# FFN and score products issued as 32-column array tiles, squares on ScalarE, and gains as rows, in a fused attention and FFN kernel

## The chip, the cores and the metric

The kernel runs on one core of one Trainium2 chip. The metric is the device time of one execution in microseconds (us), and lower is better. The kernel before takes 411.36 us, the median of 11 runs that lie between 408.41 and 414.82. A core has TensorE (matrix products; PE in the profile, with its weight loads as PEld), VectorE (DVE), ScalarE (ACT), GpSimd (POOL) and SyncE (SP, which here only starts transfers). DMA queues move data between the chip's memory and the core's buffer, SBUF. Products land in PSUM banks, from which VectorE or ScalarE take them.

## The reference, cut to what matters

```python
# q, k, v: (8, 12, 448, 64); g_q, g_k: (64,)
q_n, k_n = rmsnorm(q, g_q), rmsnorm(k, g_k)      # x / sqrt(mean(x*x) + 1e-6) * g
attn = softmax(q_n @ k_n.T / 8)                  # per batch and head
x = (attn @ v).transpose(0, 2, 1, 3).reshape(3584, 768)
a, b = x @ w1, x @ w2                            # (768, 1024) each
out = (a * b @ w3) @ w_out                       # (1024, 1024), (1024, 768)
```

All inputs and the output are 32-bit floats. Sums of squares, scales and the score exponentials are needed for every one of 96 heads; the FFN runs over 3,584 tokens.

## The kernel before, in words

**Work units.** The kernel takes four heads at a time, a *quad*: 8 batches of 3 quads, 24 quads in all. A quad takes four steps (the code's slots, `sl` 0 to 3), numbered t = 4 * quad + sl. The 448 tokens of a head stand as 112 partitions x 4. w3 and w_out are first multiplied into one matrix, w34, so that the FFN is (a * b) @ w34.

**Preparing a quad** happens up to twelve steps ahead. `load_qk` loads q and k on SP's queue (quad 0's k on ScalarE's). `prep_sq` squares q and k, in two halves of two heads: on ScalarE for quads 0 to 4 (`N_SQ_ACT = 5`), on GpSimd (L159) for the 19 others. `prep_red` sums the squares on VectorE (L166), `prep_alpha` makes exp(-0.5 ln(.)) of the sums on ScalarE (L176, L177), and `prep_scale` multiplies on VectorE: q by alpha (qtmp, L188), that by the product of the gains (L195), k by alpha (L201). The scaled halves are transposed into qkT, by TensorE for quads 0 to 4 (`N_PE_T = 5`), by a DMA transpose on SP's queue for the rest.

**A step** then does three things on TensorE. `qk_exp` makes two score tiles (sc, L235), each of two heads, as two matmuls of 64 rows by 112 columns, one in the upper and one in the lower half of the array; ScalarE makes the exponential P of each score tile (L244). sc has two PSUM buffers, so the scores of a step wait for the exponentials of the step before. `pv_set` (L259), in steps 0 to 2 of the quad that follows, makes the row sums (kind 0) or half of the value product, as four 32-column array tiles side by side, one per head, in four rounds of 448 columns. From kind 0 ScalarE makes the reciprocal r (L269, L271); VectorE multiplies kinds 1 and 2 by r into xT (L275). Last come up to two *fillers*: in steps 1 to 13 transposes of w3 (L293) and pieces of w34 (wps, L301), later units of the FFN. `ffn1_a` (pa, L315) is six matmuls of 128 x 128 against 448 columns, taken out by ScalarE as a_sb (L323); `ffn1_b` (pb, L332) is six more, multiplied with a_sb by VectorE into abT (L339). `ffn2` (po, L354) is eight matmuls against 384 columns, copied by VectorE to o_sb (L361) and stored by SP. All of these but sc share four PSUM buffers (`mm_psum`). What is left of the FFN after the last quad runs by itself at the end.

**Order.** Nothing is scheduled by a program: the order in which the code issues instructions is the order on each engine. The table `PREP` with `SHIFT` says at which step each part of a quad's preparation is issued; from quad 7 on, the squares of quad n are issued at steps 4n - 9 and 4n - 8, behind that step's exponentials, r and a_sb, the alphas one step later. `W34_SLOTS` says how many pieces of w34 stand in a step, and `LAG` how far the second half of w34's columns is behind the first.

**The start.** Sixteen matmuls on zeros warm TensorE (L393). ScalarE's queue loads quad 0's k in two halves, and then g_q and g_k, each spread to 112 partitions (L403, L404); VectorE multiplies them and by 8 into g_b (L417, L418) ahead of its first reduction. GpSimd waits in a copy (`gate`, L408) for the last half of k and then issues the weights' loads on its own, software queue: both halves of w_outs' first columns, four parts of w3s, v of quad 0, the rest of w_outs. Further loads (`wq`) follow, four issued per step.

## Time and profile before

| | |
|---|---|
| median of 11 runs | 411.36 us (408.41 to 414.82) |
| the profiled execution's own time | 410.86 us |
| its span, from the first to the last instruction | 408.7 us |
| TensorE, VectorE, ScalarE, GpSimd busy | 382.4, 288.0, 249.9, 117.4 us |
| PE instructions (matmuls and weight loads) | 6,080 |
| pa, pb, po, sc, pv matmuls | 384, 384, 448, 384, 1,152 |
| squares on ScalarE, on GpSimd | 20, 76 |
| granted TensorE clock, mean | 0.978 |
| first score exponential starts | 18.25 us |
| first FFN matmul starts | 70.9 us |

An engine's busy time is the union of its instructions' times. A weight load and a matmul are two instructions; matmuls overlap in the array, so the mean time of one (355 ns for 448 columns) is longer than the distance from one start to the next. "The chain that ended last" is followed back from the last instruction, at each point to what released it. Rows name the kernel's line, the engine, and what is written from what is read.

### The profile page before, as it was taken

Reading aid. Unit: us, or ns where it says so; the run is one execution under the profiler, and the core shown is the slowest. Engines: PE = TensorE matmul, PEld = TensorE weight load, DVE = VectorE, ACT = ScalarE, POOL = GpSimd, SP = SyncE. Lnnn points to the kernel's source line nnn. Section 1 sums busy time; section 2 is a strip of 40 time slices with the busy share of each in tenths; the row PEclk is TensorE's granted clock in tenths of the full one; section 3 lists DMA queues with packets and bytes.
Section 4 is the critical chain, followed back from the end, with each engine's and each line's share of the span. In section 5 each row is a group of like instructions: output and inputs, shape, how many; then the busy total and the mean of one; then the engine's idle time right before and its main releaser. Section 6 shows DMA issues by size and latency. Waiting matters only on the chain.

```text
span 408.7 us, 7530 instructions
## 1 busy us (share of the span) xinstructions
PE 382.4 (94%) x3040; PEld 177.3 (43%) x3040; DVE 288.0 (70%) x383; ACT 249.9 (61%) x391; POOL 117.4 (29%) x135
## 2 busy tenths in 40 slices
PE   5299999999999899998999899899999999999995
PEld 1155554444444344434444343344444444445552
DVE  0676767988978878779888878878978973234232
ACT  2479888776677646665677565674767657751210
POOL 4233434444055405504323422422532500000000
PEclk9559999999999999999999999999999999999999
DMA  6999998367795568564886487556767652003004
GB/s 198 219 233 234 197 211 153 78 103 149 189 197 79 114 149 206 112 142 67 196 170 124 80 218 120 110 136 98 191 146 155 94 143 58 0 2 115 2 19 137
DMA packets 78530, 54.61 MB, mean 134 GB/s; under 512 B 38048, under 2 KB 72352, under 8 KB 78496
## 3 DMA queue, kind: packets, MB, share of 16 engines
q1 hardware_dynamic: 61568, 41.30, 43.1%
q0 software_dynamic: 16192, 12.32, 21.2%
q10 hardware_dynamic: 736, 0.52, 0.4%
q8 instruction: 24, 0.39, 0.4%
q14 instruction: 10, 0.08, 0.1%
HBM read 46.72 MB, written 11.01 MB: 141 GB/s over the span
## 4 chain that ended last, share of the span: by engine, by line
PE 76%; DVE 10%; ACT 5%; issue 5%; DMA 3%; ACTq 0%; DVEq 0%
PE pa L315 17%; PE pb L332 16%; PE po L354 16%; PE pv L259 13%; PE sc L235 9%; PE wps L301 4%; DVE qtmp L188 2%; DMA gk_b<-in_g_k_dram 2%; DVE qks L195 2%; DVE qks L201 2%; ACT P L244 2%; ACT sq L157 1%; DVE xT L275 1%; DMA out_dram<-o_sb 1%; PE w3T_ps L293 1%
## 5 line engine op out<-in xcount | busy, mean ns | idle before, releaser
L244 ACT ACTIVATE P<-sc 112x896 bf16<-112x896 f32 x192 | 165.5, 914 | 83.6 <-PE sc L235 83.6
L159 POOL TENSOR_TENSOR sq<-q_sb 112x512 f32<-112x512 f32 x38 | 41.9, 1104 | 166.5 <-DMA q_sb<-in_q_dram 122.2
L332 PE MATMUL pb<-xT,w2s 128*128 128x448 bf16 x384 | 83.1, 352 | 2.4 <-DVE xT L275 2.4
L315 PE MATMUL pa<-xT,w1s 128*128 128x448 bf16 x384 | 84.0, 354 | 1.0 <-DVE xT L275 1.0
L354 PE MATMUL po<-w34s,abT 128*128 128x384 bf16 x448 | 78.5, 327 | 4.8 <-DVE abT L339 4.8
L339 DVE TENSOR_TENSOR abT<-pb,a_sb 128x448 bf16<-128x448 f32 x64 | 39.7, 620 | 58.5 <-PE pb L332 58.2
L166 DVE TENSOR_REDUCE ssq<-sq 112x16 f32<-112x1024 f32 x48 | 58.0, 1209 | 5.0 <-ACT sq L157 5.0
L235 PE MATMUL sc<-qkT 64*112 64x448 bf16 x384 | 58.3, 380 | 1.3 <-DVE qkT L223 0.7
L354 PEld LDWEIGHTS <-abT 128*128 128x128 bf16 x448 | 41.2, 98 | 41.4 <-issue 10.2
L323 ACT CAST a_sb<-pa 128x448 bf16<-128x448 f32 x64 | 33.9, 529 | 36.2 <-PE pa L315 36.2
L332 PEld LDWEIGHTS <-w2s 128*128 128x128 bf16 x384 | 37.6, 98 | 39.2 <-issue 4.5
L315 PEld LDWEIGHTS <-w1s 128*128 128x128 bf16 x384 | 33.0, 98 | 45.1 <-issue 20.3
L201 DVE TENSOR_TENSOR qks<-k_sb,alpha 112x512 bf16<-112x512 f32 x48 | 52.3, 1090 | 0.0
L188 DVE TENSOR_TENSOR qtmp<-q_sb,alpha 112x512 bf16<-112x512 f32 x48 | 45.9, 957 | 6.1 <-ACT alpha L177 6.0
L361 DVE COPY o_sb<-po 128x384 f32<-128x384 f32 x56 | 30.4, 553 | 25.2 <-PE po L354 25.1
L259 PE MATMUL pv<-P,v_sb 112*32 112x448 bf16 x768 | 45.1, 355 | 0.0
L159 POOL TENSOR_TENSOR sq<-k_sb 112x512 f32<-112x512 f32 x38 | 42.8, 1126 | 3.5 <-DMA k_sb<-in_k_dram 3.5
L195 DVE TENSOR_TENSOR qks<-qtmp,g_b 112x512 bf16<-112x512 bf16 x48 | 37.2, 774 | 1.7
L235 PEld LDWEIGHTS <-qkT 64*112 64x112 bf16 x384 | 17.7, 127 | 33.0 <-issue 31.1
L275 DVE TENSOR_TENSOR xT<-pv,r 128x448 bf16<-128x448 f32 x48 | 29.5, 614 | 3.6 <-PE pv L259 3.6
L259 PEld LDWEIGHTS <-v_sb 112*32 112x32 bf16 x768 | 16.1, 96 | 24.0 <-issue 15.7
L301 PE MATMUL wps<-w_outs,w3T 128*128 128x384 bf16 x128 | 24.1, 339 | 0.0
(36 smaller groups left out, 183.5 us busy)
## 6 DMA issues: line engine op xcount, KB each, us to landing
q_sb<-in_q_dram SPq DMA_DIRECT2D x23, 448.0 KB, 5.4
k_sb<-in_k_dram SPq DMA_DIRECT2D x23, 448.0 KB, 6.2
v_sb<-in_v_dram POOLq DMA_DIRECT2D x24, 224.0 KB, 4.1
out_dram<-o_sb SPq DMA_DIRECT2D x8, 336.0 KB, 3.3
out_dram<-o_sb SPq DMA_DIRECT2D x8, 288.0 KB, 2.9
w3s<-in_moe_w_dram POOLq DMA_DIRECT2D x8, 256.0 KB, 14.2
out_dram<-o_sb SPq DMA_DIRECT2D x8, 240.0 KB, 3.9
w_outs<-in_moe_w_out_dram POOLq DMA_DIRECT2D x4, 384.0 KB, 13.1
```

What stands on the lines that cost most here:

```text
L159: nc.gpsimd.tensor_tensor(out=sq[:, t], in0=src[:, hs], in1=src[:, hs], op=MULT)
L166: nc.vector.tensor_reduce(out=s["ssq"][:, :, hs, :], in_=s.pop(("sq", pr)), axis=AX, op=ADD)
L188: nc.vector.tensor_tensor(out=qtmp.transpose([0, 2, 1, 3]), in0=s["q"][:, hs], in1=alpha[:, 0, hs].unsqueeze(3).broadcast_to([NP, 2, J, D] ...
L195: nc.vector.tensor_tensor(out=qks[:, 0], in0=qtmp, in1=g_b.unsqueeze(1).unsqueeze(1).broadcast_to([NP, J, 2, D]), op=MULT,)
L201: nc.vector.tensor_tensor(out=qks[:, 1].transpose([0, 2, 1, 3]), in0=s["k"][:, hs], in1=alpha[:, 1, hs].unsqueeze(3).broadcast_to([NP, 2, ...
L235: nc.tensor.matmul(out=sc[:, u, 0:S], lhsT=qkT[u * D : (u + 1) * D, pr, J + jk, :], rhs=qkT[u * D : (u + 1) * D, pr, 0:J, :].rearrange("d ...
L244: nc.scalar.activation(out=P[:, 2 * pr : 2 * pr + 2, jk, :], in_=sc[:, :, 0:S], func=AF.Exp)
L259: nc.tensor.matmul(out=ps[h * HALF : (h + 1) * HALF, :], lhsT=w, rhs=P[:, h, jk, :], start=(jk == 0), stop=(jk == J - 1), tile_position=(0 ...
L301: nc.tensor.matmul(out=ps[:, 0:NH], lhsT=w3T[:, gc, fc * 128 : (fc + 1) * 128], rhs=w_outs[:, gc, nh * NH : (nh + 1) * NH], start=(gc == 0 ...
L315: nc.tensor.matmul(out=ps[:, 0:S], lhsT=w1s[:, c, fi * 128 : (fi + 1) * 128], rhs=xT[b][:, c, :], start=(c == 0), stop=(c == CM - 1),)
L332: nc.tensor.matmul(out=ps[:, 0:S], lhsT=w2s[:, c, fi * 128 : (fi + 1) * 128], rhs=xT[b][:, c, :], start=(c == 0), stop=(c == CM - 1),)
L354: nc.tensor.matmul(out=ps[:, 0:NH], lhsT=abT[bp][:, fi, t * 128 : (t + 1) * 128], rhs=w34s[:, fi, nh * NH : (nh + 1) * NH], start=(fi == 0 ...
```

## The change

The FFN's matmuls (pa, pb, po) are issued as four matmuls each, on the four 32-column tiles of the array, with the same moving operand; each has its own weight load. The scores are issued likewise, as tiles of 64 rows by 32 columns (the last 16 wide): a pair of heads takes eight matmuls and not two. The products that make w34, and the transposes on TensorE, stay whole. All squares go to ScalarE (`N_SQ_ACT = 24`), so that GpSimd is left with loads. The gains are loaded as one row each; VectorE multiplies them after its first reduction, a matmul with a column of ones spreads the row to 112 partitions, and VectorE copies it to g_b. GpSimd's gate waits for the first half of q. The loads on its queue come in another order (`LOADS_0`, `LOADS_1`: o is a half of w_outs' columns, in two loads, w a part of w3s, v a quad's v), and `LAG` goes from 4 to 8, so that all first halves of w34 are made ahead of the second ones. Five quads go through TensorE's transposes, as before; loads of q and k on SP keep their places.

```diff
-    N_SQ_ACT = 5
+    N_SQ_ACT = 24
-    LAG = 4
+    LAG = 8
+    LOADS_0 = ["o0", "w0", "w1", "w2", "v0", "w3", "w4"]
+    LOADS_1 = ["w5", "v1", "w6", "w7", "o1", "v2"]
+    GATE = ("q", 0)
+    QK1_AT = -1
...
-    gq_b = const.tile([NP, D], FP, name="gq_b")
-    gk_b = const.tile([NP, D], FP, name="gk_b")
+    g_row = const.tile([1, 2, D], FP, name="g_row")
+    gp_row = const.tile([1, D], BF, name="gp_row")
+    ones_row = const.tile([1, NP], BF, name="ones_row")
...
             for u in range(2):
-                nc.tensor.matmul(
-                    out=sc[:, u, 0:S],
-                    lhsT=qkT[u * D : (u + 1) * D, pr, J + jk, :],
...
+                for c0 in range(0, NP, 32):
+                    c1 = min(c0 + 32, NP)
+                    nc.tensor.matmul(
+                        out=sc[c0:c1, u, 0:S],
+                        lhsT=qkT[u * D : (u + 1) * D, pr, J + jk, c0:c1],
...
+                        tile_position=(u * D, c0),
+                    )
...
+    def narrow(ps, n, lhsT, rhs, start, stop):
+        for h in range(4):
+            nc.tensor.matmul(
+                out=ps[32 * h : 32 * h + 32, 0:n],
+                lhsT=lhsT[:, 32 * h : 32 * h + 32],
+                rhs=rhs,
+                start=start,
+                stop=stop,
+                tile_position=(0, 32 * h),
+            )
+
     def ffn1_a(b, fi):
         ps = mm_psum.tile([128, 512], FP, tag="mm", name="pa")
         for c in range(CM):
-            nc.tensor.matmul(
-                out=ps[:, 0:S],
-                lhsT=w1s[:, c, fi * 128 : (fi + 1) * 128],
-                rhs=xT[b][:, c, :],
-                start=(c == 0),
-                stop=(c == CM - 1),
+            narrow(
+                ps, S, w1s[:, c, fi * 128 : (fi + 1) * 128], xT[b][:, c, :],
+                c == 0, c == CM - 1,
             )
...
-        nc.scalar.dma_start(out=gq_b, in_=g_q.unsqueeze(0).broadcast_to([NP, D]))
-        nc.scalar.dma_start(out=gk_b, in_=g_k.unsqueeze(0).broadcast_to([NP, D]))
+        nc.scalar.dma_start(out=g_row[:, 0], in_=g_q.unsqueeze(0))
+        nc.scalar.dma_start(out=g_row[:, 1], in_=g_k.unsqueeze(0))
...
-        nc.gpsimd.tensor_copy(out=gate, in_=st[0]["k"][:, HQ - 1, 0, 0:1])
-        load_wout(0, 0)
-        load_wout(0, 1)
-        for c in range(4):
-            load_w3(c)
-        load_v(0)
-        load_wout(1, 0)
-        load_wout(1, 1)
+        if GATE is not None:
+            nc.gpsimd.tensor_copy(out=gate, in_=st[0][GATE[0]][:, GATE[1], 0, 0:1])
+        for x in LOADS_0:
+            load_any(x)
         warm(16)
-        nc.vector.tensor_tensor(out=gq_b, in0=gq_b, in1=gk_b, op=MULT)
-        nc.vector.tensor_scalar(
-            out=g_b, in0=gq_b, scalar1=8.0, scalar2=None, op0=MULT
-        )
         for pr in range(2):
             prep_sq(0, pr, on_act=True)
             prep_red(0, pr)
             prep_alpha(0, 2 * pr, 2 * pr + 2)
+            if pr == 0:
+                nc.vector.scalar_tensor_tensor(
+                    out=gp_row, in0=g_row[:, 0], scalar=8.0, in1=g_row[:, 1],
+                    op0=MULT, op1=MULT,
+                )
+                g_ps = mm_psum.tile([NP, D], FP, tag="mm", name="g_ps")
+                nc.tensor.matmul(
+                    out=g_ps, lhsT=ones_row, rhs=gp_row, start=True, stop=True
+                )
+                nc.vector.tensor_copy(out=g_b, in_=g_ps)
             prep_scale(0, pr, pe=True)
```

`ffn1_b` and `ffn2` are changed as `ffn1_a` is.

## The prediction

> **What bounds the kernel now.** I read the page's first part, then the chain of work that ended last, then stretches of that chain and the timeline around its bad places.

> ```profile
> PE 382.4 (94%) x3040; PEld 177.3 (43%) x3040; DVE 288.0 (70%) x383; ACT 249.9 (61%) x391; POOL 117.4 (29%) x135
> ...
> PE 76%; DVE 10%; ACT 5%; issue 5%; DMA 3%; ACTq 0%; DVEq 0%
> ```

> TensorE is busy 94% of the 408.7 us span, and carries 76% of the chain. So I ask first what is inside its busy time. Here is the chain of one ordinary stretch (start, length, what):

> ```profile
> 217.43 1.13 PE pb L332 x6
> 218.56 0.52 PE sc L235 x4
> 219.08 0.87 PE pv L259 x16
> 219.95 1.24 PE pa L315 x6
> 221.19 1.14 PE pb L332 x6
> ```

> Six matmuls of 448 columns take 1.14 us (189 ns each) as pb, but 1.24 as pa, which follows pv. pv is four sets of four tiles, 4 x 0.19 = 0.76, yet takes 0.87. sc is two pairs, 0.38, yet takes 0.52. So each change between the three shapes (64 rows, 32-column tiles, whole array) costs about 0.1 us. The starts of single matmuls in the trace agree: 282 to 285 ns from the last of one shape to the first of the next, 189 within one (for 384 columns 256 against 162), so 94 ns per change. The second set after a change is also late: by 11 ns in pv and FFN, by 43 in sc.

> The rest of TensorE's loss is stalls. The chain leaves it in places such as this; the timeline of the same place names the cause:

> ```profile
> 139.41 0.72 DVE qks L201
> 140.13 0.12 issue
> 140.25 0.02 DVEq L195
> 140.27 2.09 issue
> 142.36 0.61 DVE xT L275
> 142.97 0.54 DVE abT L339
> ```

> ```profile
> 138.26 1.14 DVE L195 TENSOR_TENSOR qks<-qtmp,g_b 112x512 bf16<-112x512 bf16 x1
> ...
> 139.33 3.10 DVE L201 TENSOR_TENSOR qks<-k_sb,alpha 112x512 bf16<-112x512 f32 x1
> 139.83 1.05 POOL L159 TENSOR_TENSOR sq<-q_sb 112x512 f32<-112x512 f32 x1
> ...
> 140.84 1.04 POOL L159 TENSOR_TENSOR sq<-k_sb 112x512 f32<-112x512 f32 x1
> ...
> 143.56 1.64 PE L354 MATMUL po<-w34s,abT 128*128 128x384 bf16 x9 [1.73 <-DVE abT L339]
> ```

> A key scaling that takes 0.68 us elsewhere took 3.10 with two GpSimd squares in it; abT came late, and po waited. From 70 us on TensorE has eight such gaps, together 9.5 us (1.9, 1.5, 1.3, 1.4, 1.2, 1.3, 0.9, 0.2).

> At the start VectorE's first reduction stands behind the product of the gains, which waits for g_k:

> ```profile
> 11.41 0.23 DVE L417 TENSOR_TENSOR gq_b<-gq_b,gk_b 112x64 f32<-112x64 f32 x1 [10.22 <-DMA gk_b<-in_g_k_dram]
> ...
> 11.78 1.21 DVE L166 TENSOR_REDUCE ssq<-sq 112x16 f32<-112x1024 f32 x1
> ```

> The squares it reduces were done at 5.67.

> [...]

> **The change part by part.**

> FFN as tiles. A full matmul becomes four tiles of 32 columns: per set 4 weight loads and 4 matmuls, not 1 and 1. The nearest row is pv: sets of 448 columns start 189 ns apart, as whole-array ones do, and matmuls in a set 3.4 ns apart. So array time is unchanged. What goes is the change from pv to pa or po: 63 in the trace (42 and 21), each 0.096 + 0.011: -6.7 us. Three changes from po to pv save 0.3. The 33 us after 375 have no pv, and gain nothing. PE's instructions go from 6,080 to 15,684; I cost that at nothing[...]. Uncovered, it is the rival that ends slower.

> Scores as 64x32 tiles. A pair becomes eight loads and eight matmuls. I take it that sc still drains on the way in and out, because 128x128 to 64x128, a change of rows alone, costs the same 94 ns here. Only the late second pair improves, from 43 ns towards pv's 11: 96 steps x 0.026 = -2.5 us. Bounds: 4.1 gained, or 2 lost if eight loads are slower than two. If there is no drain between the two tile modes, 69 sc-to-pv, 21 sc-to-FFN and 83 FFN-or-wps-to-sc changes go: about 170 x 0.094 = 16 us more (a rival; wps stays a whole-array product, which takes off a little).

> Squares. GpSimd loses 76 squares, ScalarE gains them. VectorE's slow cases go: up to -9.5 us of stalls. I take -8.5; the ends are -9.5 and -5, since abT also waits for ScalarE's a_sb. ScalarE pays 76 x 0.53 (start to start where two follow each other) = 40 us. Per quad, by the same measure: eight exponentials 6.5, logarithm and reciprocal 1.1, alpha 0.5, squares 2.1, 2.7 casts 1.15 = 11.3 us, against 13 to 14 for TensorE, which is the cover. But two squares stand in slot 3 and two in slot 0, where ScalarE needs 3.1 + 4.2 = 7.3 and TensorE 2.7 + 3.5 = 6.2. It falls 1.1 us behind, and recovers in slots 1 and 2 (4.6 against 6.9). Queued behind a square are the next exponentials, whose score buffers TensorE wants one step later. In the trace an exponential pair ends some 2.2 us after its scores start and the next scores come at 3.5 to 3.8, so 1.3 us of cover; it holds, narrowly. Around 61 to 88 us, where casts of w34s still run, it holds worse. I charge +3 for all (0 to +10). A square would also wait in ScalarE's order for its k: k landed from 3.7 us before to 1.5 us after the start of the step that now squares it, and the squares come about 2 us into the step, so nothing, within 0.5 us.

> Start. Gains now come as one row each behind the k halves on ScalarE's queue (k landed at 6.2, the old 112-row gains at 8.5 and 11.1), are multiplied, spread by a one-row matmul on an idle TensorE and copied, behind the first reduction. That reduction can begin at 5.7, alpha ends at 7.6, and with gains at 7 to 8.5 the first scaling starts at 8 to 9.5, not 13.61: 4 to 5.5 us. Then w3s decides: its first part landed at 20.1 and was used at 21.6. GpSimd's gate opens on the first q half (landed 4.3) and not the last k (6.2), so it starts 2 us sooner, lands near 18.2, and the gain shrinks to 3.4. The order after it (v0 before the fourth w3s, second halves of w_outs last, LAG 8 to match) leaves each part earlier than its use moved by 3.5 us. Dearer loads of q and k for quads 1 and 2 (landed 11.6 and 16.6, used from 19.9 and 28.9) have room. -3.5; bounds -1 and -5.5.

> Sum on the profiled span: 408.7 - 6.7 - 0.3 - 2.5 - 8.5 + 3 - 3.5 = 390.2. The profiled execution's time is 410.86, 2.2 above its span, so 392.4; it lies 0.5 under the median of 411.36, so I say **393 us**.

> **Rivals.**
> 1. The scores join the tile mode and drain no more: 393 - 16 = 377, of which ScalarE, then at 11.3 of 12.5 us, gives back some 2: 379. For it: all pieces would be 32 columns wide. Against: a change of rows alone costs 94 ns now.
> 2. PE's instruction supply becomes the bound: slower. From 70 to 375 us the new program has about 13,000 PE instructions (1,056 FFN sets and 63 pv groups' 252 sets of 8, 80 score steps of 32) in what were 304 us: 23.4 ns each. Above some 23.7 it loses; at 25 the stretch takes 325, and the tail (96 + 64 sets of 8 at 200 ns, not 189 and 162) 3.5 more: 408.7 + 21 + 3.5 - 3.5 + 2.7 = about 432. For it: no view shows long runs of dense PE instructions, only queued bursts of 32. Against: nothing in those bursts is slower[...].
> 3. ScalarE holds TensorE back: its slots 3 and 0 block the scores by 0.5 to 0.8 us in each of 18 quads, 9 to 14 us in place of 3: 401.

> **How the numbers follow.** Forecast 0.55 (own range 385 to 399), rival 1 0.20, rival 2 0.13, rival 3 0.09, the start and squares both failing to within 0.5% of before 0.03. A measurement here tells about 0.5% from nothing. Faster: 0.55 + 0.20 + 0.09 = 0.84; same 0.03; slower 0.13. Some 0.06 lies below 375, and above 408 the last two, so the range is 375 to 408.

> **What would show it.** Right: pv's last set to pa's first 189 ns apart, FFN sets still 189 and po's 162; about 282 into and out of sc; the scaling of k never over 0.75 us; TensorE's waits for abT under 2 us in all; first exponential near 13.5, first w3s transpose near 18. Rival 1: sc after pb at 189 too. Rival 2: FFN sets evenly above 195 ns with no semaphore named. Rival 3: waits of sc for P's exponential, 0.4 us now, of 5 us and more. The forecast is wrong if tiles' sets don't keep 189 ns over hundreds of sets, or if ScalarE's lateness comes back as late abT.

## The result and the profile after

The changed kernel takes 388.87 us, the median of 12 runs (387.24 to 390.05), against 410.69 us for the kernel before (47 runs, 406.43 to 414.96): a ratio of 0.948, with a 95% interval from 0.946 to 0.950. The forecast was 393. The profiled execution has a span of 386.5 us, 22.2 less than before.

The first part of its page and the chain that ended last:

```profile
PE 370.7 (96%) x7841; PEld 188.5 (49%) x7841; DVE 242.6 (63%) x384; ACT 284.9 (74%) x467; POOL 34.1 (9%) x59
...
PE 88%; DMA 4%; ACT 3%; DVE 2%; POOL 0%; issue 0%
```

TensorE is still the bound, and more purely: its share of the chain rises from 76 to 88%. VectorE is 45 us less busy though it lost no scaling; ScalarE gained 35 us.

Two ordinary steps of the chain (start, length, what; to be read beside the stretch from 217.43 us shown of before):

```profile
209.23 0.50 PE sc L252 x11
209.73 0.87 PE pv L277 x16
210.60 1.14 PE pa L332 x24
211.73 1.14 PE pb L332 x24
212.87 0.50 PE sc L252 x10
```

pa after pv takes 1.14 us, not 1.24: the 0.1 us that the change of shape cost is gone. "Drain" in the recorded texts is a name for this time (94 to 106 ns by single starts); what the array does in it no trace shows. The two pairs of the scores still take 0.50 us, where two sets at 189 ns would take 0.38. A step is 3.64 us, against 3.76.

The rows of the costliest groups for the scaling of k before, and for the scalings of q and k after (mean ns of one behind the comma):

```profile
L201 DVE TENSOR_TENSOR qks<-k_sb,alpha 112x512 bf16<-112x512 f32 x48 | 52.3, 1090 | 0.0
```

```profile
L203 DVE TENSOR_TENSOR qtmp<-q_sb,alpha 112x512 bf16<-112x512 f32 x48 | 32.7, 682 | 5.5 <-ACT alpha L192 5.4
L216 DVE TENSOR_TENSOR qks<-k_sb,alpha 112x512 bf16<-112x512 f32 x48 | 32.8, 684 | 0.0
```

The k scaling has a mean of 684 ns; it was 1,090. Of the 48 before, the 34 with no GpSimd square in their time took 0.68 to 0.69 us, the six with two whole squares in it 3.10 to 3.11. TensorE's waits for VectorE's results in the FFN were, before (total us, times, longest):

```profile
PE po L354 <- DVE abT L339: 4.8, 4, 1.7
PE pb L332 <- DVE xT L275: 2.4, 2, 1.3
...
PE pa L315 <- DVE xT L275: 1.0, 1, 1.0
```

The same view of the changed kernel has no such row. And the start, from the timeline:

```profile
5.80 1.22 DVE L181 TENSOR_REDUCE ssq<-sq 112x16 f32<-112x1024 f32 x1 [4.50 <-ACT sq L172]
...
8.73 0.21 DVE L440 SCALAR_TENSOR_TENSOR gp_row<-g_row 1x64 bf16<-1x64 f32 x1 [1.71 <-DMA g_row<-in_g_k_dram]
...
9.36 0.68 DVE L203 TENSOR_TENSOR qtmp<-q_sb,alpha 112x512 bf16<-112x512 f32 x1
...
18.56 1.03 PE L311 MATMUL w3T_ps<-ident,w3s 128*128 128x128 bf16 x8 [1.39 <-DMA w3s<-in_moe_w_dram]
```

The reduction began at 5.80 (11.78 before). The first scaling came at 9.36 (13.61), after VectorE had waited 1.7 us for g_k; then TensorE waited for the first part of w3s.

**Where 22.2 us came from, by the two traces.** Distances here run from the first matmul of one set to the first of the next. The first FFN matmul starts at 66.09 and not 70.89 us: 4.8. The eight gaps after it (9.5 us) are gone; TensorE has no pause above 0.4 us after 66. 63 changes from pv into the FFN fell from 295 to 189 ns, and the second set after each comes 7 ns sooner: 7.1; three changes from po to pv 0.3. Around the scores three things moved. The second pair starts 200 ns after the first, not 233 (-2.7 over 82 steps). What follows the scores starts 299 ns after their last pair, not 282 to 285 (+1.3 over 80). The scores start 292 ns after the last set of pb, not 282, and 266 after po, not 256 (+0.8 over 80). The sum is 22.3.

The last two are not longer changes of shape. The four tiles of a set start over 10 ns and a pair's eight over 21. From the last matmul of a set to the first of the next shape, the traces before and after agree: 282 to the scores from pb, 279 from the scores to pv.

### The profile page after: what moved, and what is told of

The parts are those of the page before. It is cut to its first block, busy times and chain, and to the rows that moved or that the text cites. A ratio compares the mean times of both kernels' runs of the same rounds, so it can differ in the third digit from the quotient of the medians.

```text
span 386.5 us, 17111 instructions
## 1 busy us (share of the span) xinstructions
PE 370.7 (96%) x7841; PEld 188.5 (49%) x7841; DVE 242.6 (63%) x384; ACT 284.9 (74%) x467; POOL 34.1 (9%) x59
## 4 chain that ended last, share of the span: by engine, by line
PE 88%; DMA 4%; ACT 3%; DVE 2%; POOL 0%; issue 0%
PE pa L332 19%; PE po L332 19%; PE pb L332 19%; PE pv L277 15%; PE sc L252 11%; PE wps L319 3%; DMA w3s<-in_moe_w_dram 3%; ACT P L262 1%; DMA q_sb<-in_q_dram 1%; PE w3T_ps L311 1%; ACT sq L172 1%; ACT w34s L304 1%; PE qkT_ps L235 1%; DVE qtmp L203 1%; DVE qks L216 0%; POOL w_outs L145 0%
## 5 line engine op out<-in xcount | busy, mean ns | idle before, releaser
L332 PE MATMUL pa<-xT,w1s 128*32 128x448 bf16 x1536 | 84.0, 353 | 0.0
L332 PE MATMUL pb<-xT,w2s 128*32 128x448 bf16 x1536 | 83.7, 352 | 0.0
L332 PE MATMUL po<-w34s,abT 128*32 128x384 bf16 x1792 | 78.1, 326 | 0.0
L181 DVE TENSOR_REDUCE ssq<-sq 112x16 f32<-112x1024 f32 x48 | 58.3, 1215 | 15.1 <-ACT sq L172 15.1
L332 PEld LDWEIGHTS <-abT 128*32 128x32 bf16 x1792 | 47.4, 97 | 28.0 <-issue 2.8
L252 PE MATMUL sc<-qkT 64*32 64x448 bf16 (+1 forms) x1536 | 55.9, 360 | 0.8 <-DVE qkT L238 0.7
L332 PEld LDWEIGHTS <-w1s 128*32 128x32 bf16 x1536 | 39.7, 96 | 34.4 <-issue 5.0
L332 PEld LDWEIGHTS <-w2s 128*32 128x32 bf16 x1536 | 41.0, 97 | 31.5
L125 POOL DMA_DIRECT2D v_sb<-in_v_dram x24 | 16.9, 706 | 233.4 <-PE pv L277 229.2
L216 DVE TENSOR_TENSOR qks<-k_sb,alpha 112x512 bf16<-112x512 f32 x48 | 32.8, 684 | 0.0
L172 ACT ACTIVATE sq<-q_sb 112x512 f32<-112x512 f32 x48 | 30.5, 635 | 0.7 <-DMA q_sb<-in_q_dram 0.7
L172 ACT ACTIVATE sq<-k_sb 112x512 f32<-112x512 f32 x48 | 30.0, 625 | 0.0
## 6 DMA issues: line engine op xcount, KB each, us to landing
out_dram<-o_sb SPq DMA_DIRECT2D x8, 288.0 KB, 2.8
```

Source lines behind the costliest of these rows:

```text
L172: nc.scalar.activation(out=sq[:, t], in_=src[:, hs], func=AF.Square)
L181: nc.vector.tensor_reduce(out=s["ssq"][:, :, hs, :], in_=s.pop(("sq", pr)), axis=AX, op=ADD)
L216: nc.vector.tensor_tensor(out=qks[:, 1].transpose([0, 2, 1, 3]), in0=s["k"][:, hs], in1=alpha[:, 1, hs].unsqueeze(3).broadcast_to([NP, 2, ...
L252: nc.tensor.matmul(out=sc[c0:c1, u, 0:S], lhsT=qkT[u * D : (u + 1) * D, pr, J + jk, c0:c1], rhs=qkT[u * D : (u + 1) * D, pr, 0:J, :].rearr ...
L332: nc.tensor.matmul(out=ps[32 * h : 32 * h + 32, 0:n], lhsT=lhsT[:, 32 * h : 32 * h + 32], rhs=rhs, start=start, stop=stop, tile_position=( ...
```

## The experiments

Seven kernels take one thing out of the changed kernel or put one thing into the kernel before; five probe a limit or a way to go on. Each was timed together with the kernel before, whose median lay between 410.28 and 411.59 us.

**1. FFN whole again.**

```diff
-        for h in range(4):
-            nc.tensor.matmul(out=ps[32*h : 32*h+32, 0:n], lhsT=lhsT[:, 32*h : 32*h+32], ...)
+        nc.tensor.matmul(out=ps[:, 0:n], lhsT=lhsT, rhs=rhs, start=start, stop=stop)
```

> The changed kernel with pa, pb and po as whole 128x128 matmuls again, all else kept. If the tiles gain only by the drains between pv and the FFN, 63 of them come back at 0.107 us and three from po to pv at 0.094: 388.9 + 7.0 = 396 us, and FFN sets stay 189 and 162 ns apart. If the supply of instructions was costing the tiles something out of sight, less comes back: under 393.

Measured: 394.25 us (393.94 to 395.38), ratio 0.960 (0.953 to 0.968), span 392.7, so 5.4 by medians and 6.2 by spans. Its chain has the 0.1 us between pv and pa back:

```profile
208.65 0.87 PE pv L277 x16
209.52 1.24 PE pa L331 x6
210.76 1.14 PE pb L331 x6
```

By single starts, pv to FFN is 295 again, and sets are 189 and 162 in both forms. But scores start 282 ns after the start of a whole-array set and 292 after that of a set of tiles. A step of scores, pv, pa and pb lasts 3,745 ns here and 3,641 in the changed kernel (medians of 42 steps each). In all, 63 x (0.106 + 0.007) + 3 x 0.094 - 80 x 0.010 = 6.6, and from the first FFN matmul to the end the two profiled executions differ by 6.5. So the tiles gain by the changes from pv and po, and pay 0.8 us at the scores' door; nothing else shows.

**2. Scores whole again.**

```diff
-                for c0 in range(0, NP, 32): ... tile_position=(u * D, c0)
+                nc.tensor.matmul(out=sc[:, u, 0:S], lhsT=qkT[u*D : (u+1)*D, pr, J + jk, :], ...)
```

> The changed kernel with each score product as one 64x112 matmul again. The prediction's step says +2.5 us (391.4): the second pair late by 43 ns again. The trace of the changed kernel says otherwise: the second pair is 30 ns sooner, but the first starts 10 ns later after FFN and the next shape 20 ns later after the scores, so nothing: 388.9 within 0.7.

Measured: 389.33 us (389.11 to 390.27), ratio 0.949 (0.940 to 0.957), span 387.3, 0.8 more. The second pair is at 233 ns and what follows at 282: 82 x 0.033 - 1.3 = 1.4 us. Of this, 1.1 shows in the traces from the first FFN matmul to the end, 0.8 in the spans and 0.5 in the medians. The score tiles are worth some 0.1 to 0.4%, which the times of these few runs can't tell from nothing.

**3. Squares back on GpSimd**, in the changed kernel (`N_SQ_ACT` 24 to 5).

> The changed kernel with the squares of quads 5 to 23 back on GpSimd. If they caused all eight TensorE gaps and ScalarE's 40 us more are hidden: +9.5 us, 398.4, the k scaling again at up to 3.1 us, and gaps at po or pa. If ScalarE's load costs 3 us as the prediction charged: +5.5, 394.4.

Measured: 391.93 us (388.83 to 393.98), ratio 0.954 (0.944 to 0.963): 3.1 by medians, with runs that spread over 5 us, two of them among those of the changed kernel. The profiled execution (393.96) has four gaps of together 5.2 us, as much as its span exceeds that of the changed kernel. One of them in the timeline:

```profile
119.76 3.10 DVE L216 TENSOR_TENSOR qks<-k_sb,alpha 112x512 bf16<-112x512 f32 x1
...
120.26 1.05 POOL L174 TENSOR_TENSOR sq<-q_sb 112x512 f32<-112x512 f32 x1
...
121.26 1.04 POOL L174 TENSOR_TENSOR sq<-k_sb 112x512 f32<-112x512 f32 x1
...
123.45 0.75 PE L332 MATMUL pb<-xT,w2s 128*32 128x448 bf16 x12 [1.31 <-DVE xT L293]
```

So the k scaling is as long as in the gap shown of before (3.10 us, with two squares in it), but such stalls came three times, for 4.6 us; the fourth gap, of 0.6, came 5 us after the end of one that began in step 0, with VectorE busy all the time between. VectorE's operations above 2.2 us are 12 here and 12 before; what differs is where they fall. All gaps above 1 us in both traces follow a k scaling that began in step 2 of a quad. After long operations in step 3, which has no pv, TensorE did not pause: in the trace of before five, of 2.45 to 3.03 us, are followed by no gap above 0.4. For the two short runs (388.83, 389.91) there is no profile.

**4. The old start**, in the changed kernel: gains spread by DMA ahead of the first reduction, gate on the last half of k, old order of loads, LAG 4.

> The changed kernel with the old start: gains spread by DMA, gate on the last half of k, the old order of loads, LAG 4. By the first FFN matmul (65.9 us now, 70.7 before) +4.8 us: 393.7. By the prediction's step +3.5: 392.4. First w3s transpose again near 21.4.

Measured: 391.97 us (391.41 to 393.50), ratio 0.955 (0.948 to 0.962), span 389.6: 3.1. (The recorded 65.9 and 70.7 are 66.1 and 70.9 in the views.) The first w3s transpose came at 21.19, the first FFN matmul at 69.14, 3.0 later than in the changed kernel. The old start doesn't explain the other 1.8 us to the 70.89 of before. Some 1.1 of them can be chance: in experiments 5 to 7 below, whose start is that of before, that matmul came at 69.84, 70.68 and 69.77, with TensorE's clock back at full from 28.0, 29.1 and 27.4 us (29.3 before). The rest is open.

**5 and 6. One part alone**, in the kernel before: the FFN as tiles; all squares on ScalarE.

> The kernel before with the FFN as tiles and nothing else. -7.0 us if the drains are all and a stall is not fed by the time won: 403.7 against 410.7. If a faster TensorE only waits longer for the late abT, less: down to -4 (406.7).

> The kernel before with all squares on ScalarE and nothing else. -9.5 us (401.2) if the eight gaps go and ScalarE hides the 40 us; -5.5 (405.2) if it costs 3 to 4 us.

Measured: tiles alone 397.94 us (395.40 to 401.88), ratio 0.967 (0.959 to 0.975), 12.5 less and nearly twice what the changes of shape are worth (6.6 by experiment 1). Squares alone 400.33 (399.52 to 400.79), ratio 0.974 (0.969 to 0.980), 10.1 less, with no gap above 0.5 us after 70. ScalarE's 40 us cost nothing that these times show. The two parts don't add. The profiled execution of tiles alone, the slowest of its four (401.88), has 14 VectorE operations above 2.2 us and five gaps of 8.0 us, not 9.5, again each behind a k scaling in step 2; three k scalings of 3.1 us in step 3 cost nothing. That its faster runs had fewer stalls still, though GpSimd did the same squares, fits their times; no trace shows it.

**7. When the squares fall.** If the place in the quad decides, moving the squares in time should do as well as moving them to another engine.

```diff
+                if part == "load" and n >= 8:
+                    rel = rel - 2
                 agenda.setdefault(max(0, 4 * n + rel + shift), []).append((n, part))
```

> The kernel before, all squares still on GpSimd, but q and k of quads 8 to 23 loaded two steps earlier. In the traces so far every TensorE gap above 0.7 us late in a run follows a k scaling of 2.4 to 3.1 us that began in step 2 of a quad, and long ones in step 3 cost nothing. If it is only when the squares fall, earlier loads move them off step 2 and the gaps go: 400 to 404. If GpSimd's load itself is what costs: no change, 410.

Measured: 400.23 us (399.24 to 401.47), ratio 0.980 (0.969 to 0.991): 10.1 less by medians, as in experiment 6, and 8 by the ratio. TensorE has no gap above 0.5 us after 70. By spans it is 10.7 less: 9.5 of stalls and 1.1 of an earlier first FFN matmul. Of its page:

```profile
L159 POOL TENSOR_TENSOR sq<-q_sb 112x512 f32<-112x512 f32 x38 | 39.6, 1042 | 153.5 <-DMA q_sb<-in_q_dram 81.9
...
L201 DVE TENSOR_TENSOR qks<-k_sb,alpha 112x512 bf16<-112x512 f32 x48 | 32.9, 685 | 0.0
```

GpSimd still does all 76 squares, and the k scaling is back to 685 ns. GpSimd starts its squares when q lands (the wait for q_sb ends 81.9 of the 153.5 us it is idle ahead of them); landing two steps earlier, they no longer meet a scaling from quad 8 on. So what the kernel before lost was a coincidence in time, and an edit that shifts the steps against the loads can change it. That fits experiments 3 and 5, where steps were shorter and the gaps were 5.2 and 8.0 us; the shift itself was not followed there.

**8. How much ScalarE can still hide**: each square of quads 7 to 23 done twice.

> The changed kernel with each square of quads 7 to 23 done twice on ScalarE: 68 more of 0.53 us. ScalarE then needs 13.4 us per quad, TensorE 13.1 on average, and steps 3 and 0 take it 9.4 against 6.1. If the cover is narrow as the prediction had it, TensorE waits for exponentials: +10 us or more. If ScalarE still catches up within steps 1 and 2: under +2.

Measured: 410.40 us (409.34 to 411.97), 21.5 more for 68 x 0.53 = 36 us of work. The waits of TensorE, in total, times and longest, of the changed kernel with doubled squares:

```profile
PE sc L255 <- ACT P L265: 18.9, 28, 1.0
```

The same view of the changed kernel has no such row. With squares doubled, TensorE waits at the scores in 14 quads; a quad takes 15.1 us on average, as against 13.8. So the squares as they are use cover that ends soon: of 36 us more, some 14 were hidden.

**9. How many instructions PE can be given**, and what one of them costs: each FFN product in two halves of its moving columns, the same array work by twice the FFN's instructions.

```diff
-        for c in range(CM):
-            narrow(ps, S, w1s[...], xT[b][:, c, :], c == 0, c == CM - 1)
+        for m0 in (0, S // 2):
+            for c in range(CM):
+                narrow(ps, S // 2, w1s[...], xT[b][:, c, m0 : m0 + S // 2], c == 0, c == CM - 1, m0)
```

> The changed kernel with each FFN product done in two halves of its moving columns (224 and 192), so that the same array work takes twice the FFN's instructions: about 25,400 on PE, 16 per 189 ns. [...] If it costs 12 ns or less, array time stays the bound: 390 to 396. If 22 or more, over 570.

Measured: 475.89 us (471.92 to 478.08), ratio 1.158 (1.148 to 1.167). It lies between the two, 396 and 570, but not by a cost of 12 to 22 ns that every instruction has. In the FFN's tail the chain of this kernel reads:

```profile
440.81 0.67 PE pa L332 x28
441.49 0.22 issue
441.71 0.66 PE pa L332 x20
442.37 1.15 PE pb L332 x48
443.52 1.15 PE pa L332 x48
444.67 0.29 PE pb L332 x12
444.96 0.22 issue
445.18 1.05 PE pb L332 x36
```

Between the stops 48 matmuls with their 48 loads take 1.15 us, 12 ns an instruction; the changed kernel takes 1.14 us for the same products. The stops come every 256 instructions: in the lines shown 128 matmuls, with as many loads, lie from one to the next. Numbered in order, nearly all of PE's pauses above 0.4 us from 70 us on (61 of 63, from one start to the next) stand at the same place, 187, of each 256, and together they last 79 us, of the 87 that this kernel loses to the changed one. Up to 7 of the other 8 (an estimate, half of 4 x 3.4) are TensorE's clock: it was granted at half four times for 3.4 us, each time within 1 us of the end of a pause of 2.9 to 3.7 us, while in the changed kernel it stayed full from 21.8 to 383.6 us.

The pauses end with a packet: at all 61, PE starts again 1.2 to 1.6 us after the latest packet on the instructions' DMA queue has come in. In the changed kernel the latest packet has been in for 4.0 us (median) when PE passes that place. At the 32 other places 187 of this kernel from 70 us on there is no pause above 0.4. In the stretch shown, where data queues are nearly idle (6 GB/s in that slice of the page), pauses are 0.5 us; in the middle of the kernel, where they are busy (24 to 188 GB/s), up to 3.7, though no run shows that this is the cause. Packets came 3.4 us apart at the least, and up to 7. So the limit met here is the supply of these packets, and not a fixed cost of every instruction. The rows of the DMA queue for instructions (packets of 16 KB, MB, share of 16 engines), in the changed kernel and in this one, with 38 packets more for 9,728 more PE instructions, 256 for each:

```profile
q8 instruction: 61, 1.00, 1.1%
```

```profile
q8 instruction: 99, 1.62, 1.4%
```

**10 to 12. Ways to go on**, in the changed kernel: the first part of w3s ahead of w_outs; with it the gain rows on GpSimd's queue ahead of the gate; with both, eight more warming matmuls behind the gains' product.

> The changed kernel with the first part of w3s loaded ahead of the first half of w_outs. If that part is what the start waits for (landed 18.3, TensorE ready at 17.2), the first w3s transpose comes at 17.2 and all follows 1 us sooner: 387.9. If w_outs then comes too late for the first wps, nothing: 388.9.

> As f1_w3_first, and the two gain rows loaded on GpSimd's queue ahead of its gate. VectorE waited 1.7 us for g_k. If nothing else stands behind it, another 1.7 us: 386.2. If the first w3s is by then the later of the two, only part: 387 to 388.

> As f2_w3_first_gains_gpsimd, with eight more matmuls on zeros behind the gains' product, to hold TensorE's clock, which fell to half from 11.3 to 21.5 us. If it holds: 2 us less than f2, 384 to 386. If the sparse work after it lets the clock fall all the same: as f2 or up to 1 us later.

Measured: 388.00, 388.36 and 388.42 us (386.91 to 389.51, 387.23 to 389.68, 386.62 to 389.37), so nothing that these runs can tell. The first w3s transpose came at 16.4 to 16.9, some 2 us sooner, but the first FFN matmul only at 65.8, 65.5 and 64.7 (66.1 in the changed kernel). TensorE's clock was back at full from 23.9, 23.8 and 21.7 us, and from 21.8 in the changed kernel, so a later clock may have taken back part of it; no run separates the two. In experiment 11 the gain rows landed on GpSimd's queue at 6.8 and 8.0, less than 1 us sooner. The longer warming held the full clock to 14.9 us (11.5 in the changed kernel), but it fell all the same. And each of the three profiled executions shows, from 100 us on, one or two pauses (0.5 to 1.3 us from one start to the next) that no semaphore ends; of the first, the chain:

```profile
145.62 1.14 PE po L332 x28
146.76 0.85 issue
147.61 1.65 PE po L332 x36
```

All four stand at place 187 of 256 too. The changed kernel's own profile has one there, at 146.7 us, which adds 0.2 us; PE starts again 1.4 us after a packet of instructions has come in, as in experiment 9.

## Why the prediction was right, and where not

**FFN tiles (-6.7, -0.3).** Right: sets stay at 189 and 162 ns over 1,216 sets, the change from pv falls from 295 to 189, and experiment 1 gives back 5.4 us by medians and 6.2 by spans. Two slips of the step nearly cancel. It counted the change from pv's last tile, 285 ns, against 189 from set to set; from set to set it is 295, so 106 ns a change and not 96. And it missed that scores start 10 ns later, counted from the start of the last FFN set, when that is spread over four tiles: 0.8 us in all.

**Scores (-2.5).** The mechanism was right and the size wrong. The second pair did come 33 ns sooner (26 foreseen), as pv's second set suggested, but what follows eight small tiles starts 14 to 17 ns later, since their starts are spread over 21 ns: a term the step left out. Experiment 2 shows 0.5 to 1.1 us. That changes into and out of the scores go on to cost, as the step took from the change between two shapes that differ in rows alone (94 ns before), held: 292 and 299 ns against 189, so rival 1 is out.

**Squares (-8.5, and +3 for ScalarE).** All eight gaps went (-9.5), and ScalarE's charge was nothing, where the step put 3: in the whole-kernel sum this is the largest miss, 4.0 us; the forecast was 4.1 too high, and the other misses nearly cancel. The trace of the changed kernel shows ScalarE late as foreseen: VectorE waited 20.3 us in all for a_sb, at most 1.9, but TensorE waited for none of it. That the cover holds, and narrowly, was right by experiment 8.

The step's reading of the 9.5 us was too simple, though. It took the stalls for GpSimd's price. Experiment 7 removes them with every square left on GpSimd, and experiment 3 brings only 3.1 back, in runs 5 us apart. They are the price of squares that meet a k scaling in step 2, and in this sum they belong to no one edit: taken alone, tiles give 12.5, squares 10.1 and, taken out, the start 3.1, together 25.7 for a total of 21.8. The forecast of the total stands all the same, since the changed kernel has no square left on GpSimd; its split among the parts does not.

**Start (-3.5).** Right in its terms: the first scaling came 4.25 us sooner (4 to 5.5 foreseen), w3s landed at 18.5 (18.2 foreseen, on a scale that stands some 0.25 us low against the views) and its transpose ran at 18.56. Experiment 4 gives 3.1. That w3s then decides was not right: experiment 10 moved its use by 2 us and the first FFN matmul came only 0.3 sooner. What does decide from there to the first FFN matmul is open.

**Instruction supply (rival 2).** It didn't come, but it was near. PE's instructions in the trace are 15,682, two fewer than foreseen. In experiment 9 packets of 256 PE instructions came 3.4 us apart at the best and up to 7. The changed kernel uses one in 5.2 to 6.1 us, 20 to 24 ns an instruction, which is inside that spread; so is the 23.7 ns above which rival 2 was to lose. That the step put this at nothing was the author's estimate and not shown: in the trace of before 256 PE instructions in a row took 11.1 us at the least, 43 ns each. Nor is the supply a cost of every instruction: in experiment 9 they passed at 12 ns between the stops, and stopped at 61 of 93 places 256 apart.

**Rival 3** didn't come; no wait of the scores for an exponential is listed in the changed kernel, where it put 5 us and more.

## What to carry to other kernels

On TensorE count the changes of array shape as well as the matmuls: each cost some 0.1 us here (94 to 106 ns), and giving neighbours the same tile shape removed them with the sets still at 189 and 162 ns, at the price of four times the instructions, whose supply stopped PE for 79 us in experiment 9. When a stall comes from two engines meeting, look at when in the schedule they meet before moving work away: here loads two steps earlier did about as much as taking the work off the engine. Take one part out and put one part in: the two disagreed by a factor of three for the squares, and only that showed that the gain had two owners.
